# Moving the mirrored gate and value matmuls of a fused Fourier mixing and SwiGLU kernel to the start of the next unit

## The chip, the cores and the metric

One core of a Trainium2 chip. The metric is the device time of one execution in microseconds, the median of several runs; lower is better. Engines: PE does the matmuls, ACT the activations and some copies, DVE and POOL the elementwise work, SP issues the transfers. PE writes its results to PSUM, a memory of banks that the other engines read.

## The reference, cut to what matters

```python
X = fft(fft(x, axis=1), axis=2).real          # x: 8 x 3008 x 256
g = X @ w_gate                                # 256 -> 1536
val = X @ w_val
out = (g * sigmoid(g) * val) @ w_out          # 1536 -> 256
```

## The kernel before

The kernel uses a symmetry of the transform: two output rows (a row and its mirror) share their even part P and their odd part Q. With weights Wp and Wq into which the second transform is folded, the gate of the row is Wp·P + Wq·Q; the gate of the mirrored row is Wp·P − Wq·Q. So the kernel first computes the row's gate in a PSUM bank, lets ACT read it (Silu, that is g * sigmoid(g)), and then adds Wm·Q, with Wm = −2·Wq, to the same bank: now it holds the mirrored gate. The value is done in the same way in "plain" units. In "split" units the value's even and odd parts go to two banks and DVE and POOL put the row's and the mirrored row's values together.

The columns are cut into 24 tiles of up to 512; each tile has 12 units f (12 blocks of 128 hidden features), and the output matmuls of the tile before (8 per unit, each 128x256) are put in between. Units 0, 2, 3, 5, 7 and 9 are split in tiles 2 to 20, nine units of twelve in tiles 21 and 22; all others are plain.

```python
def part_a(u):                       # row's gate and value
    g = psG.tile(...)                                    # 3 banks
    mm(g, Wp, 0, Pt, True, False); mm(g, Wq, 0, Qt, False, True)
    if split(u):
        e = psV.tile(...); mm(e, Wp, 1, Pt, True, True)      # 3 banks
        o = psV.tile(...); mm(o, Wm, 1, Qt, True, True)
        sg = sgv.tile(...)                               # 4 buffers
        nc.scalar.activation(sg, g, AF.Silu)
        # DVE: es = bc*w0 + e ; vp = es - o/2 ; vm = es + o/2 (mirrored)
        nc.gpsimd.tensor_tensor(hp, sg, vp, op=Alu.mult)
        return
    v = psV.tile(...); mm(v, Wp, 1, Pt, True, False); mm(v, Wq, 1, Qt, False, True)
    sg = sgp.tile(...)
    nc.scalar.activation(sg, g, AF.Silu)
    nc.vector.tensor_tensor(hp, sg, v, op=Alu.mult)
# [...]
def part_b(u):                       # mirrored gate, and mirrored value of a plain unit
    for gv, ps in ((0, g), (1, v))[:1 if split(u) else 2]:
        nc.tensor.matmul(ps, Wm[:, gv, ...], Qt, start=False, stop=True)
    # Silu, then the product hm on POOL (split) or DVE (plain)
# [...]
for i, u in enumerate(units):
    # [...] at f == 0 a matmul with `sel` and an ACT copy make the row bc of the tile
    part_a(u)
    if owork: owork.run(4)           # 4 output matmuls of the tile before
    if prev is not None:
        part_b(prev)
        # [...] at the end of a tile: new output work
    if owork: owork.run(4)
```

PE takes matmuls in program order, so a matmul that waits stops all of them. And the mirrored gate of a unit has to wait until Silu has read the row's gate, the mirrored value of a plain unit until DVE's product has read the row's value. In the order of before, more than one unit of PE work lies between.

## Time and profile before

| | before |
|---|---|
| median of the first 3 runs | 694.49 us (693.44 to 695.96) |
| span of the profiled run | 691.4 us |
| granted TensorE clock | 0.997 |

Lines of the page of the kernel before: busy time and share of each engine with its number of instructions; POOL's busy share in 40 slices, in tenths; and the shares of the chain of work that ended last.

```profile
PE 673.5 (97%) x4369; PEld 414.4 (60%) x4369; DVE 517.9 (75%) x925; ACT 433.4 (63%) x765; POOL 593.4 (86%) x577
...
POOL 8998999999999999999997989998999555658920
...
PE 85%; DMA 4%; DVE 4%; issue 3%; POOL 1%; SPq 1%; ACT 1%; ACTq 0%; POOLq 0%; DVEq 0%
```

PE is busy nearly all the time and is most of the chain; POOL is busy over nine tenths of most slices up to about 535 us. Two stretches of the same kernel, in the view of busy time by stretch (start and end in us, length, then PE, PEld, DVE, ACT and POOL busy us with their numbers of instructions, granted clock, DMA share, GB/s):

```profile
75.00:100.00 25.00, 20.22 (x117) 12.03 (x116) 14.03 (x22) 12.03 (x22) 24.33 (x24) 0.93 0.44 107
...
250.00:350.00 100.00, 99.63 (x644) 61.08 (x643) 77.58 (x133) 64.06 (x112) 99.42 (x92) 1.00 0.28 81
```

From 75 to 100 us POOL is full and PE loses nearly 5 us; from 250 to 350 us both are full.

PE's busy time does not say how close it is to its peak, since matmuls overlap. The start-to-start distances do. Lines of the timeline of the kernel before (start in us, duration in us, engine, line, operation, tiles and shapes, count, and in brackets the idle time before and what ended it), a plain unit:

```profile
301.48 0.38 PE L716 MATMUL g<-Qt,Wq 128*128 128x512 bf16 x1
...
301.89 0.60 ACT L743 ACTIVATE sg<-g 128x512 f32<-128x512 f32 x1 [0.21 <-PE g L716]
...
302.13 0.60 PE L676 MATMUL o<-Wo,hm 128*128 128x256 bf16 x4
...
302.52 0.69 DVE L744 TENSOR_TENSOR hp<-sg,v 128x512 bf16<-128x512 f32 x1 [1.17 <-ACT sg L743]
302.56 0.38 PE L753 MATMUL g<-Qt,Wm 128*128 128x512 bf16 x1
302.78 0.38 PE L753 MATMUL v<-Qt,Wm 128*128 128x512 bf16 x1
```

Matmuls with 512 columns start 0.21 to 0.22 us apart, four output matmuls take 0.43 to 0.44 us. The gate's second matmul starts at 301.48; Silu starts at 301.89; and the mirrored gate and value at 302.56 and 302.78 belong to the unit ahead, whose Silu is long done.

Where the kernel before waits inside the units, it is here, in unit 3 of nearly every tile (the same view):

```profile
310.16 0.68 DVE L735 SCALAR_TENSOR_TENSOR vv<-v,es 128x512 f32<-128x512 f32 x1
310.20 0.38 PE L716 MATMUL g<-Qt,Wq 128*128 128x512 bf16 x1
...
310.42 0.38 PE L716 MATMUL v<-Pt,Wp 128*128 128x512 bf16 x1
...
310.89 0.38 PE L716 MATMUL v<-Qt,Wm 128*128 128x512 bf16 x1
```

The odd part of the value of this split unit starts 0.47 us behind the even part and not 0.22: it waits for the bank that the `vv` operation of the unit before is reading until 310.84. That is 0.25 us per tile.

### The profile page before, as it was taken

The page shows a single profiled execution, that of the slowest core. Times are in us where ns is not written, and L with a number is a line of the kernel's source. Part 1 is how long each engine was busy: PE and PEld are TensorE (multiplying, and loading weights), DVE is VectorE, ACT ScalarE, POOL GpSimd, SP SyncE. Part 2 cuts the span into 40 slices and gives each one's busy share as a digit, 9 for nine tenths or more (in the row PEclk, how much of TensorE's full clock was granted, in tenths as well). Part 3 has the DMA queues.
Part 4 walks back from the last instruction along what each step waited for, and adds up shares of the span by engine and source line. Part 5 has one row for each costly group of instructions (what it writes and reads, how often), then busy time and mean ns, then how long its engine had stood idle before and what let it go on. Part 6 is the DMA issues. An engine that isn't in the chain of part 4 may idle for free.

```text
span 691.4 us, 13273 instructions
## 1 busy us (share of the span) xinstructions
PE 673.5 (97%) x4369; PEld 414.4 (60%) x4369; DVE 517.9 (75%) x925; ACT 433.4 (63%) x765; POOL 593.4 (86%) x577
## 2 busy tenths in 40 slices
PE   7999979999999999999999999999999999999997
PEld 5446645566556566566665656655665656656676
DVE  8896657677768777777777778777877787788862
ACT  7676546566556566565665656655666656656663
POOL 8998999999999999999997989998999555658920
PEclk9999999999999999999999999999999999999999
DMA  9656362332413313324134111125111011111112
GB/s 225 113 78 131 101 142 74 96 99 61 131 37 90 110 31 105 89 68 132 47 82 117 45 34 46 32 58 140 43 36 46 32 41 37 46 32 47 47 47 70
DMA packets 45567, 52.55 MB, mean 76 GB/s; under 512 B 6290, under 2 KB 33466, under 8 KB 45498
## 3 DMA queue, kind: packets, MB, share of 16 engines
q1 hardware_dynamic: 42314, 49.35, 26.2%
q0 software_dynamic: 3184, 2.36, 2.4%
q8 instruction: 34, 0.56, 0.4%
q14 instruction: 35, 0.29, 0.2%
HBM read 29.39 MB, written 24.65 MB: 78 GB/s over the span
## 4 chain that ended last, share of the span: by engine, by line
PE 85%; DMA 4%; DVE 4%; issue 3%; POOL 1%; SPq 1%; ACT 1%; ACTq 0%; POOLq 0%; DVEq 0%
PE o L676 33%; PE v L716 17%; PE g L716 15%; PE g L753 8%; PE v L753 4%; PE g L567 3%; PE v L567 3%; DVE vv L735 2%; DMA XC<-in_x_dram 2%; DMA XC_108<-in_x_dram 1%; SPq L139 1%; DMA XA<-in_x_dram 1%; DVE vv L733 1%; DMA out_dram<-ev 1%; PE g L856 1%
## 5 line engine op out<-in xcount | busy, mean ns | idle before, releaser
L736 POOL TENSOR_TENSOR hp<-sgv,vv 128x512 bf16<-128x512 f32 (+1 forms) x132 | 167.8, 1272 | 49.8 <-DVE vv L733 38.4
L758 POOL TENSOR_TENSOR hm<-sgv,vv 128x512 bf16<-128x512 f32 (+1 forms) x132 | 167.3, 1272 | 8.5 <-ACT sgv L757 8.1
L676 PE MATMUL o<-Wo,hp 128*128 128x256 bf16 (+2 forms) x1140 | 170.6, 274 | 0.0
L676 PE MATMUL o<-Wo,hm 128*128 128x256 bf16 (+2 forms) x1140 | 169.6, 273 | 0.0
L676 PEld LDWEIGHTS <-hp 128*128 128x128 bf16 (+2 forms) x1140 | 112.3, 99 | 70.9 <-issue 11.3
L676 PEld LDWEIGHTS <-hm 128*128 128x128 bf16 (+2 forms) x1140 | 111.9, 98 | 64.8 <-issue 5.5
L731 DVE SCALAR_TENSOR_TENSOR es<-bc,w_85,v 128x512 f32<-128x512 f32 (+1 forms) x132 | 98.2, 744 | 51.3 <-PE v L716 51.0
L744 DVE TENSOR_TENSOR hp<-sg,v 128x512 bf16<-128x512 f32 (+2 forms) x156 | 103.7, 665 | 31.2 <-ACT sg L743 30.8
L761 ACT ACTIVATE sg<-g 128x512 f32<-128x512 f32 (+2 forms) x156 | 91.1, 584 | 43.1 <-PE g L753 43.0
L762 DVE TENSOR_TENSOR hm<-sg,v 128x512 bf16<-128x512 f32 (+2 forms) x156 | 103.2, 662 | 18.7 <-ACT sg L761 8.6
L743 ACT ACTIVATE sg<-g 128x512 f32<-128x512 f32 (+2 forms) x156 | 90.9, 583 | 41.5 <-PE g L716 39.6
L757 ACT ACTIVATE sgv<-g 128x512 f32<-128x512 f32 (+1 forms) x132 | 78.9, 598 | 53.9 <-PE g L753 41.3
L716 PE MATMUL v<-Pt,Wp 128*128 128x512 bf16 (+2 forms) x288 | 107.9, 375 | 1.6 <-DVE vv L735 1.6
L716 PE MATMUL g<-Pt,Wp 128*128 128x512 bf16 (+2 forms) x288 | 108.3, 376 | 1.0 <-ACT sgv L757 0.9
L716 PE MATMUL g<-Qt,Wq 128*128 128x512 bf16 (+2 forms) x288 | 108.0, 375 | 0.5 <-DVE Qt L580 0.5
L753 PE MATMUL g<-Qt,Wm 128*128 128x512 bf16 (+2 forms) x288 | 108.1, 375 | 0.0
L733 DVE SCALAR_TENSOR_TENSOR vv<-v,es 128x512 f32<-128x512 f32 (+1 forms) x132 | 91.1, 690 | 22.5 <-POOL hp L736 4.6
L728 ACT ACTIVATE sgv<-g 128x512 f32<-128x512 f32 (+1 forms) x132 | 78.7, 596 | 44.8 <-PE g L716 34.9
L735 DVE SCALAR_TENSOR_TENSOR vv<-v,es 128x512 f32<-128x512 f32 (+1 forms) x132 | 89.8, 681 | 8.1 <-POOL hm L758 5.2
L716 PEld LDWEIGHTS <-Wp 128*128 128x128 bf16 x576 | 56.4, 98 | 41.1 <-issue 4.5
L682 ACT COPY ev<-o 128x512 f32<-128x512 f32 x90 | 52.8, 587 | 30.9 <-PE o L676 29.7
L153 POOL TENSOR_TENSOR SDf<-XA 128x1024 f32<-128x1024 f32 x28 | 66.0, 2364 | 3.4 <-DMA XC<-in_x_dram 2.6
(173 smaller groups left out, 736.0 us busy)
## 6 DMA issues: line engine op xcount, KB each, us to landing
out_dram<-ev SPq DMA_DIRECT2D x96, 128.0 KB
XA<-in_x_dram SPq DMA_DIRECT2D x32, 256.0 KB
XA<-in_x_dram SPq DMA_DIRECT2D x112, 64.0 KB
XC<-in_x_dram SPq DMA_DIRECT2D x105, 32.0 KB
XC<-in_x_dram SPq DMA_DIRECT2D x28, 120.0 KB
out_dram<-ev SPq DMA_DIRECT2D x12, 120.0 KB
out_dram<-ev SPq DMA_DIRECT2D x10, 112.0 KB
XA<-in_x_dram SPq DMA_DIRECT2D x1, 1024.0 KB
```

The lines of the kernel that those rows point to most:

```text
L676: nc.tensor.matmul(ps[:n, j, :], hts[minus][:, f, c:c + n], Wo[:, f, :], start=(f == 0), stop=(f == nF - 1))
L716: nc.tensor.matmul(ps[:, :w], Wt[:, gv, fs], src[:, :w], start=start, stop=stop, skip_group_check=True)
L731: stt(es[:, :w], bc[t][:, :w], w0[:, f:f + 1], e[:, :w], op0=Alu.mult, op1=Alu.add)
L733: stt(vp[:, :w], o[:, :w], -0.5, es[:, :w], op0=Alu.mult, op1=Alu.add)
L735: stt(vm[:, w - 1::-1], o[:, :w], 0.5, es[:, :w], op0=Alu.mult, op1=Alu.add)
L736: nc.gpsimd.tensor_tensor(hts[t][0][:, f, :w], sg[:, :w], vp[:, :w], op=Alu.mult)
L743: nc.scalar.activation(sg[:, :w], g[:, :w], AF.Silu)
L744: nc.vector.tensor_tensor(hts[t][0][:, f, :w], sg[:, :w], v[:, :w], op=Alu.mult)
L753: nc.tensor.matmul(ps[:, :w], Wm[:, gv, f * P:(f + 1) * P], Qt[:, :w], start=False, stop=True, skip_group_check=True)
L758: nc.gpsimd.tensor_tensor(hts[t][1][:, f, :w], sg[:, :w], v[:, :w], op=Alu.mult)
L761: nc.scalar.activation(sg[:, :w], g[:, :w], AF.Silu)
L762: nc.vector.tensor_tensor(hts[t][1][:, f, w - 1::-1], sg[:, :w], v[:, :w], op=Alu.mult)
```

## The change

Its intent is to use the mirrored matmuls as filler in the next unit and to end the lives of the gate and value banks earlier: the mirrored gate of the unit ahead comes first, then 4 output matmuls, its mirrored value, the gate and value of this unit, and 4 output matmuls. `part_b` is cut in two. No instruction is added or removed.

```diff
-    def part_b(u):
+    def mirror(u, gv, ps):           # the matmul with Wm
+    def gate_b(u):                   # mirrored gate, its Silu (and POOL product of a split unit)
+    def value_b(u):                  # mirrored value and DVE product of a plain unit
 # [...]
+        if prev is not None:
+            gate_b(prev)
+            if owork:
+                owork.run(4)
+            value_b(prev)
+            if prev[1] == nF - 1:
+                owork = OWork(prev[0], hts[prev[0]])
         part_a(u)
         if owork:
-            owork.run(4)
-        if prev is not None:
-            part_b(prev)
-            if prev[1] == nF - 1:
-                owork = OWork(prev[0], hts[prev[0]])
-                owork.run(4)
-        if owork and not (prev is not None and prev[1] == nF - 1):
             owork.run(4)
```

More of the change, by code (lines that the diff above doesn't have):

```diff
@@ L745, in part_a @@
         state[u] = (g, v)
-    def part_b(u):
+    def mirror(u, gv, ps):
         t, f = u
         w = width(t)
-        Pt, Qt = pq_tiles(t)
-        g, v = state.pop(u)
-        for gv, ps in ((0, g), (1, v))[:1 if split(u) else 2]:
-            nc.tensor.matmul(ps[:, :w], Wm[:, gv, f * P:(f + 1) * P], Qt[:, :w], start=False, stop=True,
-                             skip_group_check=True)
+        nc.tensor.matmul(ps[:, :w], Wm[:, gv, f * P:(f + 1) * P], pq_tiles(t)[1][:, :w], start=False, stop=True,
+                         skip_group_check=True)
+    def gate_b(u):
+        t, f = u
+        w = width(t)
+        g, v = state[u]
+        mirror(u, 0, g)
         if split(u):
@@ L758, in part_b @@
             nc.gpsimd.tensor_tensor(hts[t][1][:, f, :w], sg[:, :w], v[:, :w], op=Alu.mult)
-            return
-        sg = sgp.tile([P, T], F32, name="sg")
-        nc.scalar.activation(sg[:, :w], g[:, :w], AF.Silu)
-        nc.vector.tensor_tensor(hts[t][1][:, f, w - 1::-1], sg[:, :w], v[:, :w], op=Alu.mult)
+        else:
+            sg = sgp.tile([P, T], F32, name="sg")
+            nc.scalar.activation(sg[:, :w], g[:, :w], AF.Silu)
+            state[u] = (sg, v)
+    def value_b(u):
+        t, f = u
+        w = width(t)
+        sg, v = state.pop(u)
+        if not split(u):
+            mirror(u, 1, v)
+            nc.vector.tensor_tensor(hts[t][1][:, f, w - 1::-1], sg[:, :w], v[:, :w], op=Alu.mult)
     slot = {(b, part): max(first_tile[(b, part)] - 1, 0) * nF + 4 for b, part in jobs}
@@ L883 @@
         owork.run(8)
-    part_b(prev)
+    gate_b(prev)
+    value_b(prev)
     owork = OWork(prev[0], hts[prev[0]])
```

## The prediction

> What bounds the kernel now. The page's busy row gives PE 97%, POOL 86%, DVE 75%, ACT 63%; the chain of waits is 85% PE. In the PE timeline back-to-back 128x512 matmuls start 0.216 us apart and four output matmuls take 0.437 us. The Trainium skill ("TensorE: Matmul & The Clock Gate", Part 1, "Wait — 56ns, not 53.3ns?") gives 215.7 ns for N=512 warm; the trace agrees. A unit therefore costs PE 2.17 us, or 1.95 us when its value is split. Starts add up to about 653 us of streaming plus 29 us of excess. Of that excess about 10 us are small transform matmuls and 5 us the prologue, neither touched. Touched: one 0.25 us wait per tile of the second split unit's value on the vv op of the unit before (about 6 us in all), 3 us of mirrored-value waits in tile 0, and 7 us at 85-98 us, where POOL is behind. POOL is 97-99% busy from 100 to 350 us (busy time by stretches), so little could be gained there in any case. A gain over 2% (14 us) is nearly excluded.
>
> The change adds and removes no instruction. It moves the mirrored gate and value from about one unit behind their producers to 4 output matmuls behind. The skill's same page (Part 2, "Step-by-step") says matmuls stay in program order and only weight loads are pulled ahead; so a wait here stops all of PE.
>
> Costs, from the timelines. From the start of the second gate matmul (t=0), PE reaches the mirrored gate at 3x0.216+0.437 = 1.085 us. It must wait for Silu:
> - Plain unit: 0.415 (PE to ACT) + 0.60 + 0.055 (release to PE) = 1.07: just in time.
> - Split unit: 0.475 + 0.60 + 0.055 = 1.13: about 0.045 us late, x132 = 6 us.
> Mirrored value of a plain unit: PE is there at 1.735 us; gate Silu ends at 1.015, +0.035, DVE product 0.685, +0.055 = 1.79: 0.055 late, x132 = 7 us.
> ACT has no slack left: output copies (0.48 us per back-to-back op) and the bc copy now fall ahead of a gate Silu: estimate 0.09+0.15+0.08 us per tile, 5 us. DVE puts after transforms delay the next product: 2 us.
> Tile 0 has no output matmuls: without filler a unit becomes about 2.1 us instead of 1.22; some five units have no filler: +4.5 us, less the 3 us removed. Last tile +1. POOL: the split Silus ask for their 4 sgv buffers earlier, so a lagging POOL stops ACT and, at once, PE: +2 us, uncertain; slower PE gives POOL slack back.
> Removed: -6 us.
>
> Sum about +15 us: 709 us, range 697 to 720. Faster by over 2%: 3%; within 2%: 45%; slower by over 2%: 52%.
>
> To see if right: waits of PE "g L753-like mirrored gate <- ACT sgv" and "mirrored value <- DVE hp", about 0.05 us each, over a hundred times; a second gate to mirrored gate distance of 1.13 us in split units; tile 0 longer by about 1-3 us; the "v <- DVE vv" waits of 0.25 us gone; POOL's busy share down to about 84%; PE's share lower, granted clock unchanged.
>
> What would make it wrong: the latencies overlapping better than the sums (then 690-697); POOL lag turning into long PE waits through sgv (then 720 or more), visible as ACT sgv <- POOL waits of over 0.5 us in every tile; or the shorter life of g and v banks relieving the 85-98 us stall.

## The result, and the profile after

| | before | after |
|---|---|---|
| median | 693.97 us (692.89 to 695.96, 4 runs) | 713.09 us (711.29 to 714.33, 4 runs) |
| ratio | | 1.027 (95% interval 1.0236 to 1.0304) |
| span of the profiled run | 691.4 us | 710.7 us |
| granted TensorE clock | 0.997 | 0.998 |

A ratio is the mean time of one kernel's runs over that of the other's of the same rounds, so it is not quite the ratio of the medians.

The changed kernel is 2.7% slower, 19 us. Lines of its page that answer to those of before:

```profile
PE 688.2 (97%) x4369; PEld 411.9 (58%) x4369; DVE 527.4 (74%) x925; ACT 427.2 (60%) x765; POOL 593.1 (83%) x577
...
POOL 8995998899999899999997989998899645657820
...
PE 85%; DMA 4%; POOL 4%; issue 2%; SPq 2%; ACT 2%; DVE 1%; ACTq 0%; POOLq 0%; DVEq 0%
```

PE's busy time has grown by 15 us with the same 4369 matmuls: waits hidden inside a pipelined engine look like work. POOL's busy time has not changed, its share is down from 86% to 83%. The stretches (same columns); the loss in tile 2 is now at 100 to 125 us:

```profile
100.00:125.00 25.00, 22.30 (x136) 12.55 (x135) 15.38 (x32) 12.70 (x23) 21.80 (x22) 0.93 0.37 96
...
250.00:350.00 100.00, 98.89 (x626) 58.90 (x625) 75.64 (x128) 60.92 (x108) 97.27 (x91) 1.00 0.29 81
```

Where it waits. The first is a plain unit of the changed kernel, in the timeline:

```profile
319.73 0.38 PE L716 MATMUL g<-Qt,Wq 128*128 128x512 bf16 x1
...
320.14 0.60 ACT L743 ACTIVATE sg<-g 128x512 f32<-128x512 f32 x1 [0.21 <-PE g L716]
...
320.77 0.69 DVE L744 TENSOR_TENSOR hp<-sg,v 128x512 bf16<-128x512 f32 x1
...
320.81 0.38 PE L750 MATMUL g<-Qt,Wm 128*128 128x512 bf16 x1
...
321.03 0.60 PE L676 MATMUL o<-Wo,hp 128*128 128x256 bf16 x4
...
321.51 0.38 PE L750 MATMUL v<-Qt,Wm 128*128 128x512 bf16 x1
```

From the gate's second matmul (319.73) to the mirrored gate (320.81) it is 1.08 us, just what three 512-column matmuls and four output matmuls take: no wait. Silu starts 0.41 us after that matmul and ends at 320.74, DVE's product starts 0.03 us later and ends at 321.46, and the mirrored value starts 0.05 us after that, at 321.51. From the mirrored gate it is 0.70 us and not the 0.65 us that a matmul and four output matmuls take: 0.05 us lost.

Next, two split units, one after the other:

```profile
321.94 0.38 PE L716 MATMUL g<-Qt,Wq 128*128 128x512 bf16 x1
...
322.42 0.60 ACT L728 ACTIVATE sgv<-g 128x512 f32<-128x512 f32 x1 [0.59 <-PE g L716]
...
323.07 0.38 PE L750 MATMUL g<-Qt,Wm 128*128 128x512 bf16 x1
...
323.93 0.38 PE L716 MATMUL g<-Qt,Wq 128*128 128x512 bf16 x1
...
324.03 0.58 ACT L682 COPY ev<-o 128x512 f32<-128x512 f32 x1
...
324.50 0.62 ACT L728 ACTIVATE sgv<-g 128x512 f32<-128x512 f32 x1
...
325.17 0.38 PE L750 MATMUL g<-Qt,Wm 128*128 128x512 bf16 x1
```

In the first, Silu starts 0.48 us behind the gate, ends at 323.02, and the mirrored gate starts at 323.07: 1.13 us for 1.085 us of work. In the second an output copy was in ACT's way (324.03); Silu starts 0.57 us behind the gate and the mirrored gate 1.24 us behind.

The view of waits lists these poorly. All its lines of the changed kernel in which a mirrored matmul waits (engine and tile, what it waited for, us in total, times, longest us):

```profile
PE g L750 <- ACT sg L743: 5.6, 8, 2.4
...
PE v L750 <- DVE hp L744: 4.9, 9, 1.6
...
PE g L750 <- ACT sgv L728: 3.4, 5, 1.1
```

Together 22 waits. The two longest of the kernel before for its values in the same view:

```profile
PE v L716 <- DVE vv L735: 4.1, 3, 2.0
...
PE v L753 <- DVE hp L744: 2.0, 4, 0.8
```

The small waits are missing because the modelled end of the matmul before covers them. So the table that follows is made from the start-to-start distances of all matmuls: from each distance the time of the matmul is taken away (columns divided by 2400, plus 0.0025 us, which gives the 0.216 us of the timeline for 512 columns and its 0.109 us for 256), and what is left is called excess. The traces of these two kernels hold every matmul; in seven of the later runs 67 records are missing, and there the time of a missing matmul is taken away too, by aligning the trace with the program's order of instructions. The times are given to 0.01 us, so the last digit of the typical waits below means little (from times in ns, 0.043 is 0.040 and 0.153 is 0.150). The prologue is all work before the first unit.

| excess of PE starts, us | before | after |
|---|---|---|
| prologue | 9.2 | 9.8 |
| tile 0 | 5.1 | 11.0 |
| tile 1 | 0.0 | 0.5 |
| tiles 2 to 4 | 10.0 | 12.2 |
| tiles 5 to 20 | 16.9 | 25.9 |
| tiles 21, 22 | 2.7 | 3.4 |
| tile 23 and end | 0.0 | 0.5 |
| sum | 43.9 | 63.3 |

The sum differs by 19.4 us, the spans by 19.3 us: the excess explains the whole loss. About 24 us of it in both kernels are the prologue and the small transform matmuls. Within tiles 5 to 20, the typical wait (median of the 16 tiles) by unit:

| typical wait, us | before | after |
|---|---|---|
| mirrored gate, units 2, 5, 7, 9 (split) | 0 | 0.043 |
| mirrored gate, units 0, 3 (split) | 0 | 0.153 |
| mirrored gate, unit 6 (plain) | 0 | 0.153 |
| mirrored value, units 1, 8, 10 (plain) | 0 | 0.053 |
| mirrored value, unit 6 (plain) | 0 | 0.073 |
| mirrored value, units 4, 11 (plain) | 0 | 0.003 |
| odd value part, unit 3 | 0.258 | 0 |
| odd value part, unit 0 | 0.058 | 0 |

Units 4 and 11 are followed by other PE work (transform matmuls in most tiles, the `sel` matmul), which fills the time. Left out is the 0.09 us that the first matmul behind transform matmuls comes late in both kernels.

One larger loss is of another kind. Lines of the changed kernel's timeline in tile 2:

```profile
100.46 0.60 PE L676 MATMUL o<-Wo,hm 128*128 128x256 bf16 x4
100.54 1.25 POOL L762 TENSOR_TENSOR hm<-sgv,vv 128x512 bf16<-128x512 f32 x1
...
101.82 0.60 ACT L761 ACTIVATE sgv<-g 128x512 f32<-128x512 f32 x1 [2.93 <-POOL hm L762]
...
102.32 0.58 ACT L682 COPY ev<-o 128x512 f32<-128x512 f32 x1
102.78 0.62 ACT L743 ACTIVATE sg<-g 128x512 f32<-128x512 f32 x1
...
103.45 0.59 PE L750 MATMUL g<-Qt,Wm 128*128 128x512 bf16 x1 [2.39 <-ACT sg L743]
```

POOL ends a product at 101.79 and frees an sgv buffer; only then can ACT start the mirrored Silu of the unit ahead (2.93 us idle). Behind it in ACT's order stand a copy and the gate Silu of this unit, and PE's mirrored gate has waited for that Silu since 100.90, where its four output matmuls were through. So 2.55 us of PE are lost to POOL's backlog through two engines. "TensorE: Matmul & The Clock Gate" of the Trainium skill (Part 1, the paragraph "Engine queue depths") calls ACT strictly first in, first out; this sequence agrees with it. The kernel before loses nearly as much in tiles 2 to 4 (10.0 us of excess against 12.2), about half of it at its value banks. In both kernels 1.6 us of this excess are not waits: for 3.4 us after the longest gap the granted clock is 0.50 (the lines are at the end of this document).

### The profile page after: what moved, and what is told of

The parts are those of the page before. It is cut to its first block, busy times and chain, and to the rows that moved or that the text cites. A ratio compares the mean times of both kernels' runs of the same rounds, so it can differ in the third digit from the quotient of the medians.

```text
span 710.7 us, 13283 instructions
## 1 busy us (share of the span) xinstructions
PE 688.2 (97%) x4369; PEld 411.9 (58%) x4369; DVE 527.4 (74%) x925; ACT 427.2 (60%) x765; POOL 593.1 (83%) x577
## 3 DMA queue, kind: packets, MB, share of 16 engines
q1 hardware_dynamic: 42314, 49.35, 25.9%
## 4 chain that ended last, share of the span: by engine, by line
PE 85%; DMA 4%; POOL 4%; issue 2%; SPq 2%; ACT 2%; DVE 1%; ACTq 0%; POOLq 0%; DVEq 0%
PE o L676 32%; PE g L716 15%; PE v L716 15%; PE g L750 10%; PE v L750 5%; PE g L567 3%; PE v L567 3%; DMA XC<-in_x_dram 2%; POOL SDf L153 2%; DVE hp L744 1%; DMA XC_108<-in_x_dram 1%; DMA XA<-in_x_dram 1%; SPq L139 1%; ACT sg L743 1%; PE g L868 1%
## 5 line engine op out<-in xcount | busy, mean ns | idle before, releaser
L728 ACT ACTIVATE sgv<-g 128x512 f32<-128x512 f32 (+1 forms) x132 | 79.7, 604 | 46.6 <-PE g L716 36.7
L716 PEld LDWEIGHTS <-Wq 128*128 128x128 bf16 x444 | 43.2, 97 | 36.8 <-issue 0.8
```

Of the source, the lines that this page charges most:

```text
L716: nc.tensor.matmul(ps[:, :w], Wt[:, gv, fs], src[:, :w], start=start, stop=stop, skip_group_check=True)
```

## The experiments

Theory: PE now comes to a mirrored gate or value before ACT or DVE has let go of the bank; the time lost is the length of that chain less the PE work placed in between. Rival A: ACT is held by POOL through the sgv buffers. Rival B: the loss is in tile 0, where there are no output matmuls to put in between. Eleven kernels were run, all correct.

### One output matmul fewer in between

```diff
             gate_b(prev)
-                owork.run(4)
+                owork.run(5)
             value_b(prev)
 # [...]
         part_a(u)
-            owork.run(4)
+            owork.run(3)
```

> The changed order with 5 output matmuls before the mirrored value and 3 behind the gate and value, in place of 4 and 4: the mirrored gate comes 0.109 us earlier after its own gate. Theory (PE reaches the mirrored gate before Silu has read the bank): split units' wait at the mirrored gate grows from 0.04 to about 0.15 us, plain units get a new one of about 0.095 us at the mirrored gate and lose the 0.05 us at the mirrored value; +0.6 us per tile, 13 us in all: about 726 us. Rival A (the loss is POOL holding the sgv buffers): the number of output matmuls in between does not matter, within 3 us of the changed kernel's 713. Rival B (the loss is all in tile 0, which has no output matmuls): no change.

Measured: 722.99 us (722.01 to 723.43), ratio to before 1.0412 (1.0394 to 1.0429), so 1.4% slower than the changed kernel. The typical wait at the mirrored gate of units 2, 5, 7 and 9 went from 0.043 to 0.152 us, that is by 0.109 us, just the output matmul taken away; plain units 1, 8 and 10 went from 0.003 to 0.092 us and lost their 0.05 us at the mirrored value. Units 0 and 3 stayed at 0.153. A split unit in its PE timeline:

```profile
325.40 0.38 PE L716 MATMUL g<-Qt,Wq 128*128 128x512 bf16 x1
...
326.04 0.49 PE L676 MATMUL o<-Wo,hp 128*128 128x256 bf16 x3
326.52 0.38 PE L750 MATMUL g<-Qt,Wm 128*128 128x512 bf16 x1
```

The gate's second matmul starts at 325.40, the mirrored gate at 326.52: 1.12 us again, though the work between them now ends at 326.37. The distance does not follow the work; it is the chain through Silu. The wait per unit is as expected; the time was 3 us under the 726 expected. Rivals A and B, for which the number did not matter, fail.

### One output matmul more in between

```diff
             gate_b(prev)
-                owork.run(4)
+                owork.run(3)
             value_b(prev)
 # [...]
         part_a(u)
-            owork.run(4)
+            owork.run(5)
```

> 3 output matmuls before the mirrored value, 5 behind: the mirrored gate comes 0.109 us later. Theory: the 0.04 us waits of split units 2, 5, 7 and 9 go (about -3 us in all); the waits of units 0, 3 and 6 stay, since ACT (mirrored Silu, then a copy, then the gate Silu) sets them and the gate Silu is only asked for sooner; the wait at the mirrored value of plain units stays at 0.05 us since its distance from the gate is the same sum; unit 6 gets about 0.1 us worse. Net -1 to -3 us: 710 to 713 us. If distance alone counted (no ACT queue) it would be -8 us or more. Rivals A and B: no change in any of these waits.

Measured: 712.42 us (709.46 to 713.24), ratio 1.0257 (1.0232 to 1.0281), not told apart from the changed kernel's 1.027. The waits of units 2, 5, 7 and 9 are gone (0.004 us), those of units 0, 3 and 6 stay at 0.154, the mirrored value of units 1, 8 and 10 stays at 0.052, that of unit 6 goes from 0.073 to 0.182. So one output matmul more is enough where nothing is ahead of Silu on ACT, but not where ACT has a copy in hand: there the gate Silu is only asked for sooner.

### The output copies moved

```diff
             gate_b(prev)
-                owork.run(4)
+                owork.run(8 if f == 1 else 0 if f == 10 else 4)
             value_b(prev)
```

> The changed order, but 8 output matmuls before the value in unit 1 and none there in unit 10, so that the output copies of a tile fall behind the second four output matmuls of units 2, 5 and 8, after the gate Silu and not ahead of it. Theory (0.15 us at units 3 and 6 is a copy ahead of the gate Silu in ACT's order): the wait at the mirrored gate of unit 3 falls from 0.15 to about 0.04 us and of unit 6 from 0.15 to about 0; -0.28 us per tile, about -5.5 us: 707 to 709 us. Rivals: these waits stay.

Measured: 713.63 us (712.69 to 713.9), ratio 1.0279 (1.0264 to 1.0295). The time missed the 707 to 709 us expected, the waits did not: unit 3 fell from 0.153 to 0.043, unit 6 from 0.153 to 0.003 us. Unit 10, from which four output matmuls were taken, got 0.103 us at the mirrored gate and 0.213 us at the mirrored value, where it had 0.003 and 0.053. The gain of 0.26 us per tile was given back there, which I had overlooked: without them the mirrored Silu of unit 9 stands in front of the gate Silu of unit 10.

### The order of before in tile 0 only

```diff
-        if prev is not None:
-            gate_b(prev)
-            # [...]
-        part_a(u)
+        ahead = prev is not None and owork is not None
+        if ahead:
+            gate_b(prev); owork.run(4); value_b(prev)      # [...]
+        part_a(u)
+        if prev is not None and not ahead:
+            gate_b(prev); value_b(prev)                    # [...]
```

> The changed order from tile 1 on, the order of before in tile 0 (no output matmuls to stand between). Theory: the excess of PE starts in tile 0 falls from 11.0 to the 4.5 us of before, the rest keeps its waits: -6.5 us, about 706.5 us. Rival B (all of the loss is tile 0): back to 694 us. Rival A: no change.

Measured: 707.07 us (705.36 to 710.0), ratio 1.0192 (1.0164 to 1.0219). The excess of tile 0 fell from 11.0 to 5.1 us, the waits of tiles 5 to 20 stayed (26.2 us of excess against 25.9). So tile 0 is 6 of the 19 us; rival B is a part of the truth, not the whole. (The profiled spans differ by 4.9 us only, since the prologue of this run has 1.1 us more excess.)

### Six sgv buffers in place of four

```diff
-    sgv = ctx.enter_context(tc.tile_pool(name="sgv", bufs=4))
+    sgv = ctx.enter_context(tc.tile_pool(name="sgv", bufs=6))
```

> The changed kernel with 6 sgv buffers in place of 4. Theory (PE comes to the mirrored gate before Silu is done, POOL or no POOL): the typical waits of tiles 5 to 20 stay (0.043 us at units 2, 5, 7, 9; 0.15 us at 0, 3, 6; 0.05 us at the mirrored value of 1, 8, 10); only the 7.5 us of waits at the mirrored gate in tiles 2 to 4, where POOL lags, may shrink: -1 to -4 us, 709 to 712 us. Rival A (ACT held by sgv buffers that POOL has not freed): the waits at the mirrored gate go, -12 us or more, below 701 us.

Measured: 710.71 us (708.62 to 711.71), ratio 1.0226 (1.019 to 1.0262). The typical waits are those of the changed kernel to 0.002 us; the excess of tiles 2 to 4 fell from 12.2 to 9.5 us. The mirrored gates of tiles 2 to 4 wait 2.0 us in all and not 7.7, and a single wait of 1.28 us in tile 9 (told below) is gone. So rival A holds where POOL lags, for 2 to 3 us of the time, and explains nothing of the typical waits. "Perfetto Trace Analysis" of the Trainium skill (Optimization Strategy) says that a bubble that repeats can mean that buffers are short; for the repeating waits and the sgv buffers it did not here, and a run with more buffers is the cheap way to find out.

### The mirrored value behind the next gate

```diff
         ahead = ...                                   # as in the run with tile 0 in the old order
         if ahead:
             gate_b(prev)
             owork.run(4)
-            value_b(prev)
-        part_a(u)
+        part_a(u, (lambda: value_b(prev)) if ahead else None)   # called between this unit's gate and value
```

> Order of before in tile 0; from tile 1 on mirrored gate of the unit ahead, 4 output matmuls, gate of this unit, mirrored value of the unit ahead, value of this unit, 4 output matmuls. The value's distance grows by the two gate matmuls (0.43 us), the gate's by the one mirrored value (0.216 us) where the unit ahead is plain. Theory: the 0.05 us waits at the mirrored value go everywhere; the 0.043 us at the mirrored gate of units 2, 5, 7, 9 go (their unit ahead is plain); 0.13 to 0.15 us stays at units 0, 3 and 6 (ACT's queue). Against the kernel with only tile 0 restored (707): -0.4 us per tile, -8 us: about 699 us. Rival (some fixed cost of the interleaving, not the distances): no change from 707.

Measured: 701.06 us (698.89 to 703.24), ratio 1.0091 (1.0052 to 1.0129). The waits at the mirrored value are gone (0.004 us in every plain unit), those at the mirrored gate of units 2, 5, 7 and 9 too (0.003), and units 0, 3 and 6 keep 0.153: as expected unit by unit. The time is 2 us over the 699 expected, and the excess of tiles 2 to 4 is 14.3 us here.

### All eight output matmuls at the end of the unit

```diff
         if ahead:
             gate_b(prev)
-            owork.run(4)
         part_a(u, (lambda: value_b(prev)) if ahead else None)
 # [...]
         if owork:
-            owork.run(4)
+            owork.run(8)
```

> As late4, but all 8 output matmuls at the end of the unit: the mirrored gate comes at least 1.52 us behind its gate, the mirrored value at least 2.17 us, against the 1.13 and 1.79 us that the Silu and the product need, and against up to 0.3 us more where a copy is ahead in ACT's order. Theory: no waits at mirrored gate or value from tile 5 on; the 0.25 us wait per tile at the second split unit's value, which the kernel before had, stays gone; tile 0 and the POOL stall in tile 2 as in the kernel before. 687 to 690 us, so 1% faster than before. Rival (the interleaving itself costs): over 694 us.

Measured: 698.49 us (696.36 to 699.64), ratio 1.0045 (1.0003 to 1.0087): the 687 to 690 us expected was missed. The mirrored gates typically wait no more (0.007 us and less, but for the 0.09 us behind transform matmuls), and the odd value part of unit 3 neither. But a new wait of 0.244 us stands at the mirrored value of unit 1, and tiles 2 to 4 have 13.7 us of excess, not the 10 of before. The time is over the 694 us at which the rival (the interleaving itself costs) was put, but it needs no such cost: the excess is 50.0 us against 43.9 and the span 697.5 against 691.4, and it can be placed: besides the prologue (1.4 us more) and the two places just named there is a wait of 1.86 us at the mirrored gate of unit 3 in tile 9, where ACT's Silu waits for POOL. The next three runs take the first two up.

### The same, split from tile 3 on

```diff
-        return 2 <= u[0] < nT - 1 and ...
+        return 3 <= u[0] < nT - 1 and ...
```

> As late8, but values are split from tile 3 on, not from tile 2, so that POOL has 12 products (15 us) less to do while it folds. Theory (the 7 us of PE excess between 85 and 107 us, in both kernels, is POOL's backlog): that excess goes, six more 0.216 us matmuls come: -4 to -6 us against late8, 682 to 686 us. If it is not POOL: the excess stays and the run is 1 us slower than late8.

Measured: 688.73 us (688.09 to 689.43), ratio 0.9913 (0.9882 to 0.9945): 9.8 us less than the run above, where 4 to 6 were expected, and over the 682 to 686 us named. The excess of tiles 2 to 4 fell from 13.7 to 2.5 us. A part of that is clock: the trace of the run above has two stretches of 3.4 us at a granted clock of 0.50, at 91 and 111 us, and this one has none. The loss in tile 2 is POOL's backlog: with twelve products fewer there it is gone. Lines of ACT's timeline in this run, at the start of a tile, show the new wait of unit 1:

```profile
244.84 0.59 ACT L682 COPY ev<-o 128x512 f32<-128x512 f32 x1 [0.87 <-PE o L676]
245.32 0.59 ACT L873 COPY bc<-g 128x512 f32<-128x512 f32 x1
245.80 0.61 ACT L767 ACTIVATE sg<-g 128x512 f32<-128x512 f32 x1
246.29 0.62 ACT L730 ACTIVATE sgv<-g 128x512 f32<-128x512 f32 x1
```

An output copy, the bc copy, the mirrored Silu of unit 11 and the gate Silu of unit 0 come back to back; the mirrored Silu ends at 246.41, although its matmul had started at 244.85. DVE's operations come behind it in order, and its product of unit 1, for which the mirrored value waits, ends 0.05 us before that matmul starts.

### The kernel before, split from tile 3 on

The edit is the line of the run just told, made in the kernel before.

> The kernel before with values split from tile 3 on, nothing else: how much of the 688.7 us of late8_t3 is the split and how much the order. If POOL's backlog is what both kernels lose at 85 to 107 us: its excess in tiles 2 to 4 falls from 10 to about 2.5 us, six more matmuls cost 1.3 us: about 688 us, no slower than late8_t3, whose order then gains nothing on balance. If late8's order is worth something by itself: 692 us or more.

Measured: 687.63 us (687.04 to 688.73), ratio 0.9912 (0.9887 to 0.9936). This is the first of the two cases: the gain of the run above is that of the split, and the late order gains nothing on balance. The excess of tiles 2 to 4 fell from 10.0 to 3.1 us. In tiles 5 to 20 this kernel has 16.6 us of excess, the late order 18.8 us.

### The bc row made earlier, in the late order

```diff
-        if f == 0 and split((t, SPLIT[0])):
+        if f == 10 and split((t + 1, SPLIT[0])):
-            # sel matmul and bc copy of tile t
+            # sel matmul and bc copy of tile t + 1
```

(A first form in unit 8 was not run: Q of the next tile is not yet written there in every tile.)

> late8_t3 with the broadcast row of the next tile (sel matmul and the bc copy on ACT) made in unit 10 of the tile before. Theory: the 0.24 us wait per tile at the mirrored value of unit 1 is ACT's pile-up at the tile's start (output copy, bc copy, mirrored Silu, Silu back to back), which makes DVE late for the product; it falls to about 0; -4 to -5 us: 683 to 685 us, clearly below late8_t3's 688.7. If the wait is anything else, no change.

Measured: 687.95 us (687.23 to 689.17), ratio 0.9916 (0.9891 to 0.9942). The wait at the mirrored value of unit 1 fell from 0.24 to 0.004 us, so its cause was the pile-up on ACT. But the 683 to 685 us expected were missed; the time is that of the kernel before with the same split. The excess of tiles 5 to 20 fell by 2.1 us only (18.8 to 16.7), since single waits grew: the wait at unit 3 of tile 9 from 1.87 to 2.25 us, and two waits of 0.4 and 0.5 us before output matmuls of unit 1. Tiles 2 to 4 have 0.7 us more (3.2 against 2.5).

A trap of this trace: unit 4 seems to wait 0.214 us at its mirrored value. It does not. In 11 of the 16 tiles the gate's second matmul of unit 5, which comes just ahead, has no record; its weight load has one:

```profile
286.82 0.38 PE L716 MATMUL g<-Pt,Wp 128*128 128x512 bf16 x1
286.83 0.10 PEld L716 LDWEIGHTS <-Wq 128*128 128x128 bf16 x1
...
287.26 0.38 PE L752 MATMUL v<-Qt,Wm 128*128 128x512 bf16 x1
```

From 286.82 to 287.26 is the time of two matmuls, 0.43 us, with the unrecorded one in it. A false wait of just one matmul's time is the sign to look for a missing record.

### The bc row made earlier, in the changed kernel

The edit is the same, in the changed kernel.

> The changed kernel with the same move of the bc row. Theory (0.15 us at unit 0 is 0.043 for the Silu and 0.11 for the bc copy ahead of it in ACT's order): the wait at the mirrored gate of unit 0 falls from 0.153 to about 0.043 us; unit 11, which loses the sel matmul that stood between, gets 0.05 us at its mirrored value; net -0.06 us per tile, -1 us: about 712 us.

Measured: 711.83 us (710.5 to 712.68), ratio 1.0252 (1.0221 to 1.0284). The wait at unit 0 fell from 0.153 to 0.043 us, unit 11 got 0.053 us at its mirrored value: to the hundredth what the chain says. In time alone the run is not told apart from the changed kernel.

The kernel before is beaten by 0.9%, and the changed kernel by more, by the kernels that split from tile 3 on, with the order of before or the late order; the simplest of them is the kernel before with one figure changed.

## Why the prediction was right

The time (709 predicted, 713.09 measured, range 697 to 720) and the more likely side were right, and so was the mechanism. Term by term, the measured ones from the excess, some of them estimates that take tiles 5 to 20 for all:

- Mirrored gate of split units: 0.045 us each predicted, 0.043 measured (0.040 from times in ns); x132 is 5 to 6 us against 6. Shown by the two runs that moved one output matmul: the wait moved by 0.109 us, or went.
- Mirrored value of plain units: 0.055 us predicted, 0.053 measured, but at units 1, 6, 8 and 10 and in tile 1 only, as other PE work stands between at units 4 and 11; about 5.6 us against 7.
- ACT's queue: 0.09, 0.15 and 0.08 us per tile predicted, some 0.11, 0.17 and 0.11 measured (unit 3, unit 6 with its value, unit 0): about 8 us against 5. Shown by moving the output copies and the bc row, which took these waits away one by one.
- DVE puts behind transforms: 2 us predicted, nothing of it seen; unit 4, which follows them, waits 0.003 us typically.
- Tile 0: this is the term that was mis-sized. I counted +4.5 us "less the 3 us removed", so +1.5; it is +5.9 us (5.1 to 11.0), and +6 us by the run that restored it. The units without filler are six (2, 5, 6, 7, 10 and 11), not five; at their mirrored gates and values PE waits 6.4 us, where it waited 0.7. And the 3 us were not removed: PE's waits at mirrored values grew from 2.7 to 6.6 us there. The units with weight matmuls in between, which I had taken as covered, also waited (unit 0 for 1.77 us, unit 3 for 0.84 us; 0.96 us each in the kernel before), with table work in DVE's queue ahead of the product.
- POOL: +2 us predicted. Measured about 2.5: 2.2 us more excess in tiles 2 to 4, of which 1.0 us are in tiles 3 and 4 with their ordinary waits, and a wait of 1.28 us at unit 3 of tile 9, where ACT's Silu had waited 1.03 us for POOL. The run with six buffers took 2.7 us of excess from tiles 2 to 4, and the wait in tile 9.
- Last tile: +1 us predicted, 0.5 measured.
- Removed: 6 us predicted; the waits of odd value parts in tiles 5 to 22 were 7.0 us and are gone. Those of tile 2 (about 5 us) also left their place, but came back at the mirrored gates.

The measured terms give about 20 us for the 19 us measured. The predicted ones, as listed, add up to 18.5 us and not to the 15 written down. That either sum comes so near is in part luck: tile 0 and ACT's queue were some 7 us too low, and the value term, DVE's puts, the last tile and the removed waits together some 5 us too high. The base of the sum (653 us of streaming and 29 us of excess) was off as well: by the method of the table it is 643 and 43.9 us, which the forecast of a difference does not feel. In the list of what to see, "waits over a hundred times" in the view of waits was wrong: it lists 22, since it does not see a wait that the modelled end of the matmul before covers. POOL's share (84% predicted, 83% measured), the second gate to mirrored gate distance (1.13 us) and the granted clock were right. The bet that a gain was nearly excluded also held: even the order that took away all the waits at mirrored gates came out at 698.49 us as it stood.

Why Silu starts 0.06 us later behind its matmul in split units (0.475 us) than in plain ones (0.415 us) can be read in the trace. In split units ACT has a separate semaphore instruction ahead of that Silu, and this one holds the wait for PE (the Silu itself waits for POOL, for its buffer). A line of the view of L728 of the changed kernel (durations in ns, least, median and greatest):

```profile
L728 ACTq EVENT_SEMAPHORE  x130: 17/17/17, 90.6 to 676.7; - x130
```

In units 2, 5, 7 and 9 of tiles 5 to 20 it comes 0.413 us (median) behind the start of the gate's second matmul, as late as Silu itself comes in plain units, and Silu 0.062 us behind it. In plain units the separate instruction waits for DVE, is through before the matmul, and Silu holds the wait for PE. So the chain of a split unit is 1.13 us and not 1.07, and its wait of 0.04 us goes back to this. No run moved that wait to test it.

What stays open: why the late order has more excess in tile 2 than the order of before.

## What to carry to other kernels

When a matmul must wait until another engine has read its bank, add up the whole chain behind that bank (start of the matmul to start of the reader, the reader, its release, and what stands ahead of it in the reader's own queue) and compare it with the PE work in program order in between; a shortfall of 0.05 us in each of 288 units is 2% of such a kernel. Read this from start-to-start distances, since the waits can hide in PE's busy time (15 us more here). And look for stages that lack the filler (here the first tile, without output matmuls): they pay the whole chain.

## What the Trainium skill lacked or had wrong

- Delays from one engine to another: "Perfetto Trace Analysis" (Summary: the profiler window per engine type) says that semaphore propagation is hidden from the profile; no page has numbers for these pairs. Here, from the start of a 512-column matmul to the start of ACT on its bank it was 0.415 or 0.475 us (the matmul as recorded is 0.38 of that); from the end of ACT as recorded to DVE 0.03 us, to PE 0.05 us; from the end of DVE to PE 0.05 us.
- "Perfetto Trace Analysis" (Identifying the Most-Contended Engine) warns that matmul busy time says little about the roofline; it does not say that it rises with waits. Here it rose from 673.5 to 688.2 us with the same matmuls.
- "TensorE: Matmul & The Clock Gate" (Part 1, What's actually happening) gives the step of the clock down to a half after at least one idle window of about 3.4 us. Here the step came at 103.4 us, at the end of a gap of PE of 2.55 us (shorter gaps had gone before it); PE was still at work for 0.9 of the 3.4 us before the step. The length of the gap alone does not decide: gaps of 3.3 us (output copies moved, 93.2 to 96.6 us) and 2.9 us (six sgv buffers, 101.3 to 104.1 us) passed with the clock at 1.00. Lines of the view of busy time by stretch of the changed kernel (granted clock is the third figure from the end):

```profile
103.00:104.00 1.00, 0.55 (x2) 0.26 (x2) 0.57 (x1) 0.40 (x1) 1.00 (x2) 0.71 0.53 118
104.00:105.00 1.00, 1.00 (x6) 0.60 (x4) 0.12 (x1) 0.60 (x1) 1.00 (x3) 0.50 0.73 204
...
107.00:108.00 1.00, 1.00 (x10) 0.80 (x9) 0.87 (x2) 0.26 (x1) 1.00 (x2) 1.00 1.08 301
```

  The granted clock is 0.50 after the gap and 1.00 again 3.4 us later; the 512-column matmuls in between start 0.43 us apart. The kernel before does the same at 90 to 93 us, after a gap of 2.1 us.
- The strict order of matmuls and the 0.216 us ("TensorE: Matmul & The Clock Gate", Part 1, the section on 56 ns, and Part 2) agree with all runs.
